# Sliding-window attention and a token mixer on one core: tails of the first batch loaded apart, scores in two-bank units, all PSUM banks shared, and a stored instruction order

## The chip, the core and the metric

The kernel runs on one core of one Trainium2 chip. A time is device microseconds (us) of one execution; the profile is one execution under the hardware profiler, and its span is some 1.8 us shorter than the time of that execution. Engines: PE (matmul), PEld (weight load, overlaps PE), ACT (ScalarE), DVE (VectorE), POOL (GpSimd), SP (the queue that issues most DMAs here). "Slow" here is a run more than 1.5% above the fastest of the same kernel. Only fast runs are compared. A ratio is the mean time of one kernel's fast runs over that of the other's fast runs of the same rounds, so it is not quite the ratio of the medians that are quoted beside it.

## The reference

Eight batches, eight heads, 576 positions, head size 64, float32 inputs.

```python
scores = q @ k.T / 8 + slopes[h] * -(i - j)        # only 0 <= i - j < 128, else -1e9
attn   = softmax(scores)
x      = (attn @ v) as [batch, 576, 512]            # heads side by side
wq, wk = x @ w_q, x @ w_k                           # 512 -> 64
mixed  = (wq @ wk.T / 8) @ x                        # over the 576 tokens
out    = relu(mixed) @ w_out
```

The 576 positions are four blocks of 128 and a *tail* of 64.

## The kernel before

Everything is an operation with a name, the engines that may run it, a priority, and what it reads and writes. A list scheduler with a cost table orders the operations when the kernel is built; the order of each engine is then fixed. Names used below: S (scores of a head pair), E (exponential), M (product with the bias table), PV (values), N (normalising), XT (transpose of x), WK, WQ, G, MX, R (the mixer; R is its relu), O and Oe (output product and its copy from PSUM).

PSUM has eight banks. They are allocated as four tiles of two banks each:

```python
pairs = [pp.tile([P, 1024], FP32, name=f"bank{i}") for i in range(4)]
def bank(b):
    return pairs[b // 2][:, 512 * (b % 2) : 512 * (b % 2) + 512]
```

The scores of a pair of heads take banks 0 to 3 as one unit; each head's exponential reads two of them. All other work but the mixing shares banks 4 to 7:

```python
def banks_for(o, t):
    ...
    if n == 4:
        return (0, 1, 2, 3) if all(ok[0:4]) else None
    if n == 2:
        return next(((b, b + 1) for b in pool if b % 2 == 0 and ok[b] and ok[b + 1]), None)
    free_ = [b for b in pool if ok[b]]
    return next(((b,) for b in free_ if not ok[b ^ 1]), (free_[0],) if free_ else None)
...
op({"PE": 0.48}, f"S{b}{c}", ..., opens=(key, 4, None), mode="R")
for i in range(2):
    op({"ACT": 0.95}, f"E{b}{c}{i}", ...)          # pt[.., i, 0:1024] = exp(pairs[i] / 8)
```

Inputs go through six load buffers (`ld`, 512 KB each), are cast to half precision by POOL, transposed by PE and copied to SBUF. The tails of all eight batches are loaded at the start, and batch 0 needs them:

```python
for b in range(NB):                                 # x: q, k, v
    nc.sync.dma_start(out=ldtail[x][16 * b : 16 * b + 16],       # 16 partitions
                      in_=srcs[x][b, :, 512:576, :].rearrange("h (g j) d -> g h (j d)", j=4))
```

The softmax here doesn't subtract the row's maximum and nothing guards it: scores larger than these inputs give would overflow.

Of the kernel before, what the change touches and what calls it, by code (L numbers as in the profile page):

```python
# [13 lines left out]
P = 128  # L15
# [13 lines left out]
PE_SWITCH = {("F", "R"): 0.12, ("R", "F"): 0.16, ("F", "C"): 0.12, ("C", "F"): 0.16,  # L29
             ("R", "C"): 0.15, ("C", "R"): 0.15}  # L30
LAT = {"PE": 0.25, "ACT": 0.12, "DVE": 0.12, "POOL": 0.15, "SP": 0.1}
MODE_PEN = 0.6
# [3 lines left out]
class Op:  # L36

# [3 lines left out]
    def __init__(self, engs, name, prio, fn, reads=(), writes=(), after=(), opens=None, psum=None,  # L41
                 mode="F", dma=0.0, lag=0.0):
        self.engs, self.name, self.prio, self.fn = engs, name, prio, fn
        self.reads, self.writes, self.after = list(reads), list(writes), list(after)
        self.opens, self.psum, self.mode, self.dma, self.lag = opens, psum, mode, dma, lag
        self.deps, self.room, self.memory = {}, set(), {}
        self.banks = self.eng = None
        self.insts = []


def plan(ops, rings):
# [25 lines left out]
    for us in users.values():  # L77
        opener = [o for o in us if o.opens][0]
        for o in us:
            if o is not opener:  # L80

                opener.deps.update({n: d for n, d in o.deps.items() if n in o.room})
                o.deps[opener.name] = o.memory[opener.name] = opener
    left = {k: len(v) for k, v in users.items()}
    bank_free, bank_user, where = [0.0] * 8, [None] * 8, {}
    n_deps = {o.name: len(o.deps) for o in ops}
    succ = {}
    for o in ops:
        for d in o.deps:
            succ.setdefault(d, []).append(o)  # L90
    engines = ("PE", "ACT", "DVE", "POOL", "SP")
    ready = {e: [] for e in engines}

    def release(o):
        for e in o.engs:
            ready[e].append(o)
    for o in ops:
        o.ready = {e: 0.0 for e in o.engs}
        if not o.deps:
            release(o)  # L100
    free = dict.fromkeys(engines, 0.0)
    mode, dma_free, t, order = "F", 0.0, 0.0, []

    def banks_for(o, t):
        _, n, pool = o.opens
        ok = [bank_user[b] is None and bank_free[b] <= t + 1e-9 for b in range(8)]
        if n == 4:
            return (0, 1, 2, 3) if all(ok[0:4]) else None
        if n == 2:
            return next(((b, b + 1) for b in pool if b % 2 == 0 and ok[b] and ok[b + 1]), None)  # L110
        free_ = [b for b in pool if ok[b]]
        return next(((b,) for b in free_ if not ok[b ^ 1]), (free_[0],) if free_ else None)

    while len(order) < len(ops):
        moved = False
        for e in engines:
            if free[e] > t + 1e-9:
                continue
            best = None
            for o in ready[e]:  # L120
                pr = o.prio + (MODE_PEN if e == "PE" and o.mode != mode else 0.0)
                if o.ready[e] > t + 1e-9 or best is not None and pr >= best[0]:
                    continue
                if o.opens and banks_for(o, t) is None:
                    continue
                best = (pr, o)
            if best is None:
                continue
            o = best[1]
            for e2 in o.engs:  # L130
                ready[e2].remove(o)
            o.eng, o.start = e, t
            if e == "PE" and o.mode != mode:
                o.start += PE_SWITCH[mode, o.mode]
                mode = o.mode
            o.end = free[e] = o.start + o.engs[e]
            o.done = o.end
            if o.dma:
                dma_free = max(o.end + 1.0, dma_free) + o.dma
                o.done = dma_free + 0.9  # L140
            if o.opens:
                where[o.psum] = banks_for(o, t)
                for b in where[o.psum]:
                    bank_user[b] = o.psum
            if o.psum:
                o.banks = where[o.psum]
                left[o.psum] -= 1
                if left[o.psum] == 0:
                    for b in o.banks:
                        bank_user[b], bank_free[b] = None, o.done + LAT[e]  # L150
            order.append(o)
            for s in succ.get(o.name, []):
                for e2 in s.engs:
                    lag = o.lag if e2 == e and not o.dma else LAT["SP" if o.dma else e]
                    s.ready[e2] = max(s.ready[e2], o.done + lag)
                n_deps[s.name] -= 1
                if n_deps[s.name] == 0:
                    release(s)
            moved = True
        if not moved:  # L160
            times = [free[e] for e in engines] + bank_free
            times += [o.ready[e] for e in engines for o in ready[e]]
            later = [x for x in times if x > t + 1e-9]
            if not later:
                raise RuntimeError("stuck: " + str([o.name for e in ready for o in ready[e]][:20]))
            t = min(later)
    order.sort(key=lambda o: o.start)
    return order


# [76 lines left out]
def steps(nc, pool, pp, q, k, v, moe_w_q, moe_w_k, moe_w_out, out):  # L247
# [5 lines left out]
    def bank(b):  # L253
# [32 lines left out]

    ptf = pt.rearrange("p a i w -> p (a i w)").bitcast(FP32)
    ldtail = [ptf[:, 2048 * i : 2048 * i + 2048].rearrange("p (h w) -> p h w", h=H) for i in range(2)]
    ldtail.append(rm.rearrange("p i c w -> p (i c w)").bitcast(FP32).rearrange(
        "p (h w) -> p h w", h=H))  # L290
    nattail = [osb[i].rearrange("p t w -> p (t w)").bitcast(F16).rearrange(
        "p (a j h d) -> p a j h d", a=2, j=4, h=4) for i in range(2)]
# [45 lines left out]
    def f_ones(eng, bk):  # L338
# [3 lines left out]
        nc.vector.memset(vtail[64:128], 0.0)  # L342

# [6 lines left out]
    op({"DVE": 1.1}, "k zero", -98, lambda eng, bk: nc.vector.memset(kTt, 0.0), writes=[("kzero", 0)])  # L350
    op({"DVE": 1.5}, "ones", -15, f_ones, writes=[("ones", 0)])
    op({"DVE": 0.3}, "zero", -14, f_zero, writes=[("zero", 0)])
    op({"DVE": 0.2}, "pads", -10, f_pads, after=["cast qt", "cast kt"], writes=[("pads", 0)])
# [16 lines left out]
    op({"POOL": 3.2}, "load w", 12, f_w, writes=[("w", 0)], dma=1.0)  # L370
# [5 lines left out]
    srcs, loads = (q, k, v), []  # L376
    for b in range(NB):
        base = b * PERIOD
        for hh in range(2):
            for x in range(3):  # L380
                pr = (base - 14 + 2 * hh * SLOT + x * 0.3, base - 9 + hh * SLOT)[x == 2]
                loads.append((pr, b, x, hh))
    for i, (pr, b, x, hh) in enumerate(sorted(loads)):
        t = ld[i % RINGS["ld"]]

        def f_load(eng, bk, b=b, x=x, hh=hh, t=t):
            src = srcs[x][b, 4 * hh : 4 * hh + 4, 0:512, :].rearrange(
                "h (g j) d -> g h (j d)", j=4)
            nc.sync.dma_start(out=t, in_=src)

        def f_cast(eng, bk, b=b, x=x, hh=hh, t=t):
            dst = vn[b % 2][:, :, 4 * hh : 4 * hh + 4, 0:64]
            if x < 2:
                dst = nat[(4 * b + 2 * hh + x) % RINGS["nat"]]
            copy(eng, dst, in_order(t))
        name = f"{'qkv'[x]}{b}{hh}"
        op({"SP": 0.45}, "ld " + name, pr - 4, f_load, writes=[("ld", i)], dma=1.4)
        engs = {"POOL": 1.1}
        if b == 0 and x < 2:
            engs = {"POOL": 1.1, "DVE": 1.1, "ACT": 0.95}  # L400
        op(engs, "cast " + name, pr, f_cast, reads=[("ld", i)] + [("ones", 0)] * (x == 2),
           writes=[("vn", b) if x == 2 else ("nat", 4 * b + 2 * hh + x)])
    for x in range(3):
        for b in range(NB):
            def f_loadt(eng, bk, x=x, b=b):
                (nc.scalar if eng == "ACT" else nc.sync).dma_start(
                    out=ldtail[x][16 * b : 16 * b + 16],
                    in_=srcs[x][b, :, 512:576, :].rearrange("h (g j) d -> g h (j d)", j=4))
            op({("ACT", "SP", "SP")[x]: 0.45}, f"ld {'qkv'[x]}t{b}", (-50, -17.5, -12.5)[x], f_loadt,
               writes=[("ldt", x)], dma=0.35)  # L410

        def f_castt(eng, bk, x=x):
            for hh in range(2):
                src = in_order(ldtail[x][:, 4 * hh : 4 * hh + 4])
                if x < 2:
                    copy(eng, nattail[x][:, hh], src)
                else:
                    copy(eng, vntail[:, :, 4 * hh : 4 * hh + 4, 0:64], src)
        name = f"{'qkv'[x]}t"
        op({"POOL": 2.2, "DVE": 2.2} if x < 2 else {"POOL": 2.2}, "cast " + name,  # L420
           (-13, -12.8, -5)[x], f_castt, reads=[("ldt", x), ("ones", 0)], writes=[("natt", x)])
    for b in range(NB):
        for kb in range(NT):
            def f_hop(eng, bk, b=b, kb=kb):
                src = vn[b % 2][32 * kb : 32 * kb + 32].rearrange("p j h d -> p j (h d)")
                nc.sync.dma_start(out=vt[b % 2][:, kb, :], in_=src)
            op({"SP": 0.45}, f"hop{b}{kb}", b * PERIOD - 4.5 + SLOT, f_hop, reads=[("vn", b)],
               writes=[("vt", b)], dma=0.4)

# [315 lines left out]
```

## Time and profile before

| | before |
|---|---|
| time, median of 2 runs | 232.6 us (231.56 and 233.64) |
| span of the profile | 230.8 us |
| first WK result ("wkn") copied out, batch 0 | 63.7 us |
| last "wkn", batch 7 | 212.9 us |
| mean step from one "wkn" to the next | 21.3 us |
| last "wkn" to the end | 17.9 us |

"wkn" is the result of the mixer's first projection; its DVE copy marks the point where a batch's attention is done. The next lines are from the page's second part: the span in 40 slices of 5.8 us; digits are busy tenths, DMA is the busy share of the DMA engines, GB/s what they moved.

```profile
PE   0012615687676787498859977886989598774560
...
DMA  6999999999999976997899730182065026015026
GB/s 142 179 162 182 213 262 347 288 320 323 352 347 344 348 223 162 358 349 208 250 354 296 181 98 3 44 196 83 4 151 127 0 73 160 0 27 158 0 71 156
```

The DMA engines are shown busy from the second slice on, yet the first five slices move about half of what later ones move, and PE is busy for little more than a quarter of the time until slice 8 (46 us; slices are counted from 0). The windows view gives each engine's busy time in the three stretches, start, steady part and end:

```profile
core 0: us, PE busy (x) PEld busy (x) DVE busy (x) ACT busy (x) POOL busy (x), PEclk, DMA share, GB/s
0.00:64.00 64.00, 26.96 (x361) 22.03 (x362) 31.86 (x53) 32.83 (x42) 28.56 (x40) 0.92 1.11 253
64.00:213.00 149.00, 115.98 (x1527) 76.54 (x1521) 85.03 (x145) 93.61 (x150) 35.05 (x30) 0.92 0.60 175
213.00:230.80 17.80, 6.94 (x38) 2.78 (x38) 0.92 (x2) 5.95 (x14) 0.00 (x0) 0.88 0.29 74
```

In the steady part no engine is full: PE is busy for 116 of 149 us. The tile view of the banks for ACT in that stretch says what ACT's idle time ended with (us, times):

```profile
its engine sat idle before it (us, times) until:
  PE bank L186: 34.2, 30
  DVE xT L186: 13.0, 8
```

The end of the timeline (start, duration, engine, operation, and in brackets the idle time before it and what ended that):

```profile
218.29 1.89 PE L186 MATMUL bank<-wout_sb,rm 128*128 128x512 f16 x8 [1.60 <-ACT rmt L186]
...
220.21 0.59 ACT L186 COPY osb<-bank 128x512 f32<-128x512 f32 x1 [1.37 <-PE bank L186]
220.85 1.02 PE L186 MATMUL bank<-wout_sb,rmt 128*128 128x512 f16 x4 [0.67 <-ACT osb L186]
221.91 0.59 ACT L186 COPY osb<-bank 128x512 f32<-128x512 f32 x1 [1.11 <-PE bank L186]
```

Two output products (x8) are done by 220.2.

### The profile page before, as it was taken

The page shows a single profiled execution, that of the slowest core. Times are in us where ns is not written, and L with a number is a line of the kernel's source. Part 1 is how long each engine was busy: PE and PEld are TensorE (multiplying, and loading weights), DVE is VectorE, ACT ScalarE, POOL GpSimd, SP SyncE. Part 2 cuts the span into 40 slices and gives each one's busy share as a digit, 9 for nine tenths or more (in the row PEclk, how much of TensorE's full clock was granted, in tenths as well). Part 3 has the DMA queues.
Part 4 walks back from the last instruction along what each step waited for, and adds up shares of the span by engine and source line. Part 5 has one row for each costly group of instructions (what it writes and reads, how often), then busy time and mean ns, then how long its engine had stood idle before and what let it go on. Part 6 is the DMA issues. An engine that isn't in the chain of part 4 may idle for free.

```text
span 230.8 us, 4775 instructions
## 1 busy us (share of the span) xinstructions
PE 149.9 (65%) x1920; PEld 101.4 (44%) x1920; DVE 117.8 (51%) x198; ACT 132.4 (57%) x206; POOL 63.6 (28%) x69
## 2 busy tenths in 40 slices
PE   0012615687676787498859977886989598774560
PEld 0011504476545465255545655563556356333220
DVE  6101727459893387323780786386278648244000
ACT  0059654745655566925582749854785895821531
POOL 6400524747575660670093035000000000000000
PEclk9999999659998899959995999999799999799996
DMA  6999999999999976997899730182065026015026
GB/s 142 179 162 182 213 262 347 288 320 323 352 347 344 348 223 162 358 349 208 250 354 296 181 98 3 44 196 83 4 151 127 0 73 160 0 27 158 0 71 156
DMA packets 41414, 43.51 MB, mean 189 GB/s; under 512 B 4016, under 2 KB 36784, under 8 KB 41392
## 3 DMA queue, kind: packets, MB, share of 16 engines
q1 hardware_dynamic: 38656, 41.50, 65.5%
q0 software_dynamic: 1584, 0.66, 3.1%
q10 hardware_dynamic: 1152, 1.05, 2.9%
q8 instruction: 15, 0.25, 0.4%
q14 instruction: 7, 0.06, 0.1%
HBM read 29.62 MB, written 9.44 MB: 169 GB/s over the span
## 4 chain that ended last, share of the span: by engine, by line
PE 38%; ACT 20%; DMA 18%; DVE 17%; issue 3%; POOL 1%; SPq 0%; ACTq 0%; DVEq 0%
PE bank L186 38%; DMA pt<-in_k_dram 9%; ACT pt L186 5%; ACT rm L186 5%; ACT osb L186 4%; ACT kT L186 4%; DVE x L186 4%; DVE pt L186 4%; DMA ld<-in_q_dram 3%; DVE xT L186 3%; DMA ld<-in_k_dram 3%; DMA rm<-in_v_dram 3%; DVE qT L186 3%; DVE wkn L186 2%; DVE inv L186 1%
## 5 line engine op out<-in xcount | busy, mean ns | idle before, releaser
L186 ACT ACTIVATE pt<-bank 128x1024 f16<-128x1024 f32 x64 | 63.0, 1030 | 22.0 <-PE bank L186 21.6
L186 DVE TENSOR_TENSOR pt<-pt,table 128x2048 f16<-128x2048 f16 x32 | 41.5, 1297 | 11.1 <-ACT pt L186 10.9
L186 PE MATMUL bank<-ident,nat 128*128 128x128 f16 x256 | 22.9, 246 | 35.1 <-ACT nat L186 16.7
L186 PE MATMUL bank<-wout_sb,rm 128*128 128x512 f16 x128 | 37.3, 423 | 10.3 <-ACT kT L186 5.1
L186 POOL CAST nat<-ld 128x1024 f16<-128x1024 f32 x28 | 34.3, 1228 | 32.5 <-PE bank L186 14.5
L186 PEld LDWEIGHTS <-nat 128*128 128x128 f16 x256 | 18.9, 110 | 38.0 <-ACT nat L186 16.9
L186 ACT COPY osb<-bank 128x512 f32<-128x512 f32 x32 | 18.6, 592 | 26.2 <-PE bank L186 19.6
L186 DVE COPY xT<-bank 128x576 f16<-128x576 f16 x32 | 14.5, 454 | 31.7 <-PE bank L186 24.4
L186 DVE TENSOR_TENSOR x<-bank,inv 128x640 f16<-128x640 f32 x32 | 26.4, 824 | 1.1
L186 POOL CAST vn<-ld 128x1024 f16<-128x1024 f32 x16 | 19.4, 1212 | 22.1 <-DMA vt<-vn 11.0
L186 PEld LDWEIGHTS <-pt 128*128 128x128 f16 x576 | 22.6, 103 | 5.4 <-issue 4.0
L186 PE MATMUL bank<-vt,pt 128*128 128x65 f16 x512 | 23.8, 201 | 1.1 <-ACT osb L186 0.7
L186 PEld LDWEIGHTS <-rm 128*128 128x128 f16 x128 | 12.9, 105 | 24.2 <-issue 15.3
L186 PE MATMUL bank<-ident,x 128*128 128x128 f16 x160 | 15.6, 233 | 10.9 <-DVE x L186 3.7
L186 ACT COPY kT<-bank 128x1024 f16<-128x1024 f16 x16 | 16.7, 1043 | 10.2 <-PE bank L186 4.7
L186 PE MATMUL bank<-qT,kT 64*128 64x256 f16 (+1 forms) x256 | 21.1, 282 | 1.0 <-ACT pt L186 0.9
L186 DVE COPY qT<-bank 128x512 f16<-128x512 f16 x32 | 12.0, 418 | 18.8 <-PE bank L186 18.8
L186 PEld LDWEIGHTS <-x 128*128 128x128 f16 x160 | 11.4, 104 | 19.1 <-issue 9.3
L186 ACT ACTIVATE rm<-bank 128x512 f16<-128x512 f32 x32 | 19.3, 620 | 0.6 <-PE bank L186 0.6
L186 PEld LDWEIGHTS <-kT 64*128 64x128 f16 x320 | 14.5, 101 | 8.8 <-issue 5.2
L186 DVE RECIPROCAL inv<-bank 128x10 f32<-128x10 f32 x32 | 6.9, 217 | 15.6 <-PE bank L186 15.1
L186 PE MATMUL bank<-wqT,gm 64*128 64x256 f16 x64 | 8.4, 295 | 7.0 <-ACT rmt L186 2.5
(49 smaller groups left out, 136.7 us busy)
## 6 DMA issues: line engine op xcount, KB each, us to landing
ld<-in_q_dram SPq DMA_DIRECT2D x16, 512.0 KB, 7.3
ld<-in_k_dram SPq DMA_DIRECT2D x16, 512.0 KB, 7.8
ld<-in_v_dram SPq DMA_DIRECT2D x16, 512.0 KB, 7.3
out_dram<-osb SPq DMA_DIRECT2D x64, 128.0 KB, 2.3
vt<-vn SPq DMA_DIRECT2D x32, 130.0 KB, 3.9
pt<-in_q_dram ACTq DMA_DIRECT2D x8, 128.0 KB, 9.6
pt<-in_k_dram SPq DMA_DIRECT2D x8, 128.0 KB, 9.4
rm<-in_v_dram SPq DMA_DIRECT2D x8, 128.0 KB, 6.9
```

The costliest lines, as they stand in the source:

```text
L186: r = call(*a, **k)
```

## The change

Its intent: let batch 0 start without the tails of all batches; let the scores double-buffer and use whatever PSUM is free; divide the copies out of PSUM between ACT and DVE; and store an order found by a search instead of running the list scheduler. Core of the diff, cuts marked:

```diff
-def plan(ops, rings):  ... list scheduler ...
+def planned(ops):                       # the order and the banks are a stored string
+    for item in PLAN.split():           # "281A6": operation 281 on ACT; digit: first bank
+        n, e, b = re.fullmatch(r"(\d+)([PADGS])(\d?)", item).groups()
+        ...
 # scores
-            op({"PE": 0.48}, f"S{b}{c}", ..., opens=(key, 4, None), mode="R")
-            # E{i}: pt[.., i, 0:1024] from two fixed banks
+            for u in range(2):          # key blocks 0-1, then 2-4, of both heads
+                op({"PE": 0.24}, f"S{b}{c}{u}", ..., opens=(key, 2), mode="R")
+                # E{u}: pt[.., both heads, 512 columns] from any pair
 # batch 0's own tails, 0.4 MB
+        (nc.scalar if eng == "ACT" else nc.sync).dma_start(
+            out=ldn[x][0:64], in_=srcs[x][0, :, 512:576, :].rearrange("h s d -> s h d"))
 # the other tails: with batch 1, one head of all batches per transfer, 128 partitions
-            out=ldtail[x][16 * b : 16 * b + 16],
-            in_=srcs[x][b, :, 512:576, :].rearrange("h (g j) d -> g h (j d)", j=4))
+            out=t[:, h, :], in_=srcs[x][:, 4 * hh + h, 512:576, :].rearrange(
+                "b (g j) d -> g b (j d)", j=4))
-    op({"POOL": 3.2}, "load w", 12, f_w, ..., dma=1.0)
+    op({"POOL": 3.2}, "load w", 12, f_w, after=["cast k01"], ..., dma=4.0)
 # DVE may evict too: relu R, outputs Oe and OTe, k
-            op({"ACT": 0.62}, f"R{b}{db}", ...)
+            op({"ACT": 0.59, "DVE": 0.75}, f"R{b}{db}", ...)
 # each POOL cast waits for the last bias product M
+            tc.add_manual_dep(o.insts[0], bias.insts[0].name, ..., reason="port")
```

## The prediction

> **What bounds the kernel before** (timeline, unless said).
>
> 1. *Start, 0 to 64 us* (64: first mixing projection, "wkn", of batch 0). DMA binds: its engines are shown 99% busy from slice 1 on. But slices 0 to 4 move 142 to 213 GB/s, later ones 320 to 350. The packets show why: while the 64-row tails of all eight batches stream (24 transfers of 128 KB, each into 16 partitions), a 1024-byte packet takes 92 to 112 ns (median); from 30 us on, 48 to 58. The tails hold up everything: first exponential at 29.9 us, second pair at 37.7, first value product at 48.6.
> 2. *Steady, 64 to 213 us*: "wkn" at 64, 89, 112, 134, 156, 175, 194, 213: 21.3 us a batch. PE is busy 116 of these 149 us and idles 33, 25 of them in gaps over 0.5 us. ACT waits for PE's banks 34 us in 30 waits (tile view of the banks). ACT and DVE are 55 to 75% busy (windows view). No engine is full: they wait on each other in turn. One cause: a pair's scores take four fixed banks, and both exponentials (1.03 us each) must end before the next pair's scores start; everything else shares the other four.
> 3. *End, 213 to 231 us*: output of the last batch, mostly serial.
>
> **The change.** Engine work stays: 64 exponentials of 1024 columns, 32 bias products, the same matmuls plus 8 small transposes. By my count the tiling mode changes 99 times before, 95 after (the Trainium skill, "TensorEngine Tiling (Array Packing)", Key Properties: a mode change drains the array), so smaller score units cost nothing there. Removed: batch 0's wait for all tails (0.4 MB first, the rest with batch 1, spread over 128 partitions, so I expect full-rate packets); the early weight load; the bank split; ACT's monopoly of evictions (9 of 32 relus, 8 of 36 output copies, 3 of 16 k evictions go to DVE). Added: each POOL cast waits for the last bias product, which took 1.34 us while POOL ran and 1.22 after; at most 3 us are in this.
>
> **Cost.** *Start*: "wkn" of batch 0 needs about 10.4 MB; at 330 GB/s plus 2 to 3 us that is 34 us, then cast, transposes, eviction, scores, exponential: 6. ACT needs 10 us of tables (from 6 us) + 16.5 (exponentials) + 4 (evictions): also near 38. I expect 42: minus 22. *Steady*: DVE needs about 15.5 us a batch, ACT 14.5, PE 16.7. A searched order with free banks should reach 18.5, against 21.3: 7 x 2.8 = minus 20. *End*: copies and relus over two engines: 15 instead of 17.8: minus 3. Sum: 42 + 130 + 15 = 187 us span, plus 1.8 between span and time, plus 1 for what a fixed order loses.
>
> Predicted: 190 us, range 180 to 202. Faster by over 2%: 0.97, within 2%: 0.02, slower: 0.01.
>
> **What would show it.** Right: slices 1 to 5 above 280 GB/s; first exponential at 14 to 18 us; "wkn" of batch 0 at 38 to 46; 17.5 to 19.5 us between "wkn"s; ACT's waits for banks between first and last "wkn" halved; last "wkn" to end 14 to 16 us. Wrong: tails still at 90 ns a packet; a steady period near 21 us with PE idle 20%, which would say that banks were not what held it.
>
> **What would make it wrong.** The steady period is the weakest term: each microsecond there is 7. The denser PE may be granted a lower clock (0.92 on average now), or the order may stall on late DMA in batches 1 and 2.

## The result, and the profile after

190.7 us, median of 2 fast runs (190.62 and 190.79); ratio to before 0.8199, 95% interval 0.8041 to 0.8357. The total came within 1 us of the prediction. Its three parts did not:

| part of the span | before | predicted | after |
|---|---|---|---|
| start: to the first "wkn" | 63.7 | 42 | 49.3 |
| steady: first to last "wkn" | 149.2 (21.3 a batch) | 130 (18.5) | 117.1 (16.7) |
| end: last "wkn" to the end | 17.9 | 15 | 22.6 |

The lines that answer to those of before, the slices of 4.7 us now:

```profile
PE   0339549548686999978888999988988988976740
...
DMA  4996999999799879999889999998664216273564
GB/s 134 289 338 176 253 276 292 237 250 273 183 323 329 219 218 340 307 320 328 265 215 357 320 309 294 324 332 274 163 154 119 55 33 194 47 185 104 150 173 121
```

The windows view of the three stretches:

```profile
0.00:49.00 49.00, 27.32 (x320) 20.49 (x320) 26.98 (x47) 29.63 (x40) 25.57 (x41) 0.80 0.95 250
49.00:166.00 117.00, 102.29 (x1547) 71.11 (x1546) 95.19 (x173) 83.00 (x124) 36.88 (x37) 0.98 0.80 242
166.00:189.10 23.10, 11.96 (x64) 4.65 (x62) 2.49 (x5) 7.59 (x16) 0.00 (x0) 0.93 0.56 143
```

PE does the work of the steady part (about the same number of matmuls, 1547 and 1527) in 117 us and is busy for 102 of them. So of the 32 us that went, 18 were idle time of PE (33 to 15) and 14 busy time (116 to 102), with a granted clock of 0.98 and not 0.92 in that stretch; section 1 comes back to the clock. ACT's waits between first and last "wkn":

```profile
its engine sat idle before it (us, times) until:
  PE bank L163: 18.7, 25
  DVE osb L163: 4.7, 1
  DVE xT L163: 3.2, 4
```

The wait for PE's banks is about halved, from 34.2 to 18.7 us. The start stayed at 250 GB/s although its packets were now fast. What the DMA queue on SP waited for in the first 50 us:

```profile
SPq L163 <- POOL vn L163: 4.0, 2, 3.6
SPq L163 <- POOL vntail L163: 3.6, 1, 3.6
SPq L163 <- DVE nat L163: 3.3, 1, 3.3
SPq L163 <- DMA ld<-in_q_dram: 3.0, 2, 2.1
SPq L163 <- POOL nat L163: 2.2, 2, 1.6
```

POOL's and DVE's casts (13.1 us of these) are what frees a load buffer. So for 13 of the first 50 us the loads stood still for lack of buffers, not for lack of bandwidth. The end, finally:

```profile
174.43 1.89 PE L163 MATMUL bank<-wout_sb,rm 128*128 128x512 f16 x8 [0.61 <-DVE osbt L163]
176.36 0.58 ACT L163 COPY osb<-bank 128x512 f32<-128x512 f32 x1 [1.78 <-PE bank L163]
...
176.99 1.02 PE L163 MATMUL bank<-wout_sb,rm 128*128 128x512 f16 x4 [0.67 <-ACT osb L163]
178.05 0.58 ACT L163 COPY osb<-bank 128x512 f32<-128x512 f32 x1 [1.11 <-PE bank L163]
178.69 1.02 PE L163 MATMUL bank<-wout_sb,rmt 128*128 128x512 f16 x4 [0.67 <-ACT osb L163]
179.75 0.58 ACT L163 COPY osb<-bank 128x512 f32<-128x512 f32 x1 [1.11 <-PE bank L163]
```

These products stand alternately in banks 2 and 3. The semaphore values in the built program, condensed, PE's counter in brackets:

```
PE   product O(6,2) -> bank 2
PE   product O(7,1) -> bank 3                 [1912]
ACT  copy of bank 2            waits for PE [1912]     the product in bank 3
PE   product O(7,0) -> bank 2  waits for ACT's copy of bank 2              [1916]
ACT  copy of bank 3            waits for PE [1916]     the product in bank 2
```

The copy of bank 2 waits for a product in bank 3 and the other way round. The two banks are halves of one PSUM tile, and the waits come out as if the tile were one piece of memory. By a count over the whole program, 159 of the 522 waits between instructions that touch PSUM have their other end in the partner bank only; before the change it is 167 of 512. Some of these also carry data through SBUF (46 of the 159 and 56 of the 167 go to an instruction that reads what the other one wrote), the rest guard nothing. I call the rest *false waits*.

### The profile page after: what moved, and what is told of

It is laid out like the page before. It is cut to its first block, busy times and chain, and to the rows that moved or that the text cites. A ratio compares the mean times of both kernels' runs of the same rounds, so it can differ in the third digit from the quotient of the medians.

```text
span 189.1 us, 4795 instructions
## 1 busy us (share of the span) xinstructions
PE 141.6 (75%) x1928; PEld 96.3 (51%) x1928; DVE 124.7 (66%) x225; ACT 120.2 (64%) x180; POOL 62.5 (33%) x76
## 4 chain that ended last, share of the span: by engine, by line
PE 34%; DVE 24%; DMA 16%; ACT 13%; issue 4%; SPq 3%; POOL 1%; ACTq 1%; DVEq 0%; POOLq 0%
PE bank L163 34%; DVE pt L163 6%; DVE x L163 5%; DMA ldn<-in_q_dram 4%; ACT kT L163 4%; DVE xT L163 4%; DMA ld<-in_k_dram 4%; ACT osb L163 3%; DMA vt<-vn 3%; DMA out_dram<-osb 3%; SPq L163 3%; DVE qT L163 3%; ACT rm L163 3%; DMA ld<-in_q_dram 2%; DVE wkn L163 2%
## 5 line engine op out<-in xcount | busy, mean ns | idle before, releaser
L163 PE MATMUL bank<-wout_sb,rm 128*128 128x512 f16 x128 | 31.7, 379 | 4.7 <-ACT osb L163 1.3
L163 PE MATMUL bank<-ident,nat 128*128 128x128 f16 x288 | 26.1, 248 | 9.8 <-POOL nat L163 2.7
L163 ACT COPY osb<-bank 128x512 f32<-128x512 f32 x26 | 14.9, 589 | 23.0 <-PE bank L163 14.5
L163 PEld LDWEIGHTS <-nat 128*128 128x128 f16 x288 | 21.2, 111 | 14.7 <-issue 8.2
L163 PE MATMUL bank<-qT,kT 64*128 64x256 f16 (+1 forms) x256 | 23.2, 277 | 5.0 <-ACT kT L163 1.5
L163 POOL CAST vn<-ld 128x1024 f16<-128x1024 f32 x16 | 16.8, 1057 | 20.1 <-DMA ld<-in_v_dram 11.5
L163 ACT COPY kT<-bank 128x1024 f16<-128x1024 f16 x13 | 13.4, 1028 | 9.4 <-PE bank L163 8.9
L163 PE MATMUL bank<-ident,x 128*128 128x128 f16 x160 | 13.0, 222 | 4.9 <-DVE qT L163 3.6
L163 ACT ACTIVATE rm<-bank 128x512 f16<-128x512 f32 x23 | 13.8, 604 | 4.0 <-PE bank L163 3.8
L163 PE MATMUL bank<-x,wkn 128*64 128x512 f16 x80 | 10.1, 380 | 1.5 <-DVE osb L163 0.9
```

Of the source, the lines that this page charges most:

```text
L163: r = call(*a, **k)
```

## The experiments

All kernels gave correct results. Fast means below are means of the fast runs.

| run | what | fast runs | fast mean | ratio to before |
|---|---|---|---|---|
| before_spread | before, tails over 128 partitions | 2 | 222.4 | none given (231.8 for before) |
| before_nopair | before without false waits | 2 | 203.6 | none given |
| list_old | tails apart (with the later weight load and POOL's wait of the change); scores, banks, evictions and scheduler as before | 2 | 210.8 | 0.9088 (0.8956 to 0.922) |
| list_old_np | the same without false waits | 4 | 198.3 | 0.8596 (0.845 to 0.8741) |
| list_new | the change, order by the list scheduler | 2 | 198.6 | 0.8618 (0.847 to 0.8767) |
| list_new_np | the same without false waits | 4 | 181.4 | none given |
| the change | | 2 | 190.7 | 0.8199 (0.8041 to 0.8357) |
| noport | the change without POOL's added wait | 2 | 190.4 | 0.8212 (0.8107 to 0.8317) |
| nopair | the change without false waits | 3 | 177.6 | 0.7659 (0.7569 to 0.7748) |
| plan_act_np | nopair, evictions back on ACT | 4 | 182.4 | 0.7801 (0.7736 to 0.7866) |
| plan_split_np | nopair, scores in banks 0-3 only | 4 | 198.3 | none given |
| plan_pair_np | the same, one pair at a time | 4 | 210.1 | none given |
| np_ld8 | nopair with eight load buffers | 6 | 174.8 | 0.7585 (0.7521 to 0.7649) |

No ratio is given for some runs, mostly because only one run of before in their rounds was fast (228.8 us, the others 233 to 237). The differences read from those runs are larger than that, except the 3.8 us between `list_new_np` and `nopair`. The rows come from different chips, so a difference of a few us between two rows is not exact.

### 1. The false waits taken away

The edit goes after the order is made. It declares, for users of the two different banks of a pair on different engines, that there is nothing to wait for; waits that carry data stay. Operations that hold two banks are left out; by the count above, 53 of 568 waits still have their other end in the partner bank only in `nopair`, and 41 of 563 in `before_nopair`. `before_nopair` has the same edit on the kernel before.

```diff
     drop_implied(tc, order)
+    apart(tc, order)
+def apart(tc, order):
+    last = {}
+    for o in order:
+        if not o.banks or len(o.banks) > 1:
+            continue
+        for d in last.get(o.banks[0] ^ 1, [])[-12:]:
+            if d.name not in o.deps and d.eng != o.eng:
+                for i in o.insts:
+                    for j in d.insts:
+                        tc.declare_no_dep(i, j, reason="another bank")
+        last.setdefault(o.banks[0], []).append(o)
```

> The changed kernel, with the waits taken away that the built program has between users of the two different banks of one PSUM pair (the data never meet). In the trace of the changed kernel the last five output products each wait 0.67 us for the copy before, because the copy of one bank starts only when the product in the other bank of its pair has ended. Theory (these waits are false and cost time): those five gaps go, minus 3.3 us at the end, and a few us more in the middle: 183 to 188 us against 190.7. Rival (the engines are full and the waits only show where the slack is): at the end 3 us less at most, in all 188 to 190.7.

Measured: 177.6 us against 190.7, a gain of 13 where I had thought of 3 to 8. "wkn" of batch 0 came at 46.9 us, the steady step was 16.1 us, the end 18.0 us (its profile fell in a run 1% above the fast mean, so these are a little long). The end shows it best; these lines are from the timeline of the run with eight load buffers (section 5), which has the same end:

```profile
160.56 2.76 PE L163 MATMUL bank<-wout_sb,rm 128*128 128x512 f16 x12
...
161.63 0.58 ACT L163 COPY osb<-bank 128x512 f32<-128x512 f32 x1 [0.23 <-PE bank L163]
...
162.50 0.58 ACT L163 COPY osb<-bank 128x512 f32<-128x512 f32 x1 [0.28 <-PE bank L163]
163.16 1.03 PE L163 MATMUL bank<-wout_sb,rmt 128*128 128x512 f16 x4
163.36 0.58 ACT L163 COPY osb<-bank 128x512 f32<-128x512 f32 x1 [0.28 <-PE bank L163]
```

PE no longer has any bracket: it runs product after product, and each copy follows its own product. In the changed kernel's end PE stood for 5.1 us in eight gaps: four of 0.67 us before the last output products (the expectation says five) and four of 0.58 to 0.68 us before earlier products. All eight are gone here, and the end went from 22.6 to 18.0 us.

> The kernel before without the false waits between the two banks of a pair. There all work but the scores sits in banks 4 to 7, so in two pairs, and a bank whose partner is in use is taken first. Theory (the false waits cost it as much as they cost the new kernel, 10 to 13 us): 219 to 224 us against 232, and PE's gaps smaller. Rival (they became dear only through the sharing of all banks): 229 to 233 us.

Measured: 203.6 us, against 228.8 for the one fast run of before in these rounds and 231.8 on average before them. So the false waits cost the old kernel some 25 to 28 us, more than they cost the new one (13). The theory named their kind rightly and put their size at half. The trace has the steady step at 17.4 us in place of 21.3, while the first "wkn" stays at 62.7 and the end at 18.0 us. Its steady stretch in the windows view:

```profile
63.00:185.00 122.00, 105.91 (x1520) 70.19 (x1516) 84.79 (x145) 92.08 (x150) 35.78 (x31) 0.97 0.72 217
```

So **of the 4.6 us a batch by which the change shortened the steady part, 3.9 could be had in the old kernel by dropping waits alone.** My prediction named the fixed banks and the exponentials that must end as the cause of these gaps.

A rival is the granted clock, which is 0.97 in this stretch and 0.92 in the kernel before; PE is busy for 106 us with as many matmuls, not 116. But `list_old` (section 2), with its false waits in place, was granted 0.99 in its steady stretch (44 to 190 us), and there PE still idled for 34 us and the step was 20.9 us. So a higher clock alone does not shorten the step; why the clock differs is not shown. In the end of `before_nopair` the three gaps of 0.67 us are gone as well, but the clock there was 0.70 (0.88 before) and PE was busy for 10.7 us with 46 matmuls (6.9 us with 38 before), which took the gain back.

### 2. The tails: how many partitions, and loading them apart

```diff
-    out=ldtail[x][16 * b : 16 * b + 16], in_=srcs[x][b, :, 512:576, :]...("h (g j) d -> g h (j d)")
+    out=ldtail[x][:, b, :],              in_=srcs[x][:, b, 512:576, :]...("b (g j) d -> g b (j d)")
     # cut: the two places that read the tails follow the new layout
```

> The kernel before, only that each tail transfer fills 4 rows of 16 tokens in all 128 partitions (one head of all batches) and not 16 partitions (one batch, all heads); number, bytes and 1 KB packets stay. Theory (the 16 partitions are what made the packets slow): packets of 46 to 60 ns in the first 30 us and not 92 to 112, first exponential at 22 to 26 us and not 29.9, wkn of batch 0 at 54 to 59 and not 64, 223 to 228 us. Rival (the slow packets come of too many small loads or of the cold start of the run): packets still about 90 ns, 231 to 233 us.

Measured: 222.4 us against 231.8, a little better than the expected 223 to 228. A 1024-byte packet took these medians, by stretches of 5 us:

```
                0-5   5-10  10-15  15-20  20-25  25-30 us
before           46    102    112     96     92    100 ns
before_spread    46     59     59     46     46     47 ns
```

The first exponential came at 24 us and not at 29.9, "wkn" of batch 0 at 57 and not at 63.7. The Trainium skill, "SBUF — State Buffer", Door 1, says that DMA bandwidth depends on how many of 16 ports the partitions of a transfer reach, and by its table 16 neighbouring partitions reach four. This run agrees in kind: the bytes, the number of transfers and the packet size are the same, the partitions changed (and with them which tails go in one transfer), and packets became about twice as fast.

`list_old` keeps this and loads batch 0's tails apart, all as in the change, but has the scores, banks, evictions and scheduler of before:

```diff
-            for u in range(2): ... op({"PE": 0.24}, f"S{b}{c}{u}", opens=(key, 2)) ...
+            op({"PE": 0.48}, f"S{b}{c}", ..., opens=(key, 4, None))     # as before
-   opens=(key, 1)          +   opens=(key, 1, range(4, 8))             # as before
-   order = planned(ops)    +   order = the list scheduler of before
```

> The tails apart alone: the changed kernel's loads and batch 0's own tails, but the scores in four fixed banks, the other work in the other four, evictions on the engines of before and the order from the list scheduler of before. Theory (the start is worth its own share and the steady period keeps 21 us): wkn of batch 0 at 45 to 50 us, 20.5 to 21.5 us a batch after, 214 to 219 us. Rival (what the start gains is given back, as the next batches wait for their loads): 224 to 232 us.

Measured: 210.8 us, ratio 0.9088, below the expected 214 to 219: half of the whole gain. "wkn" of batch 0 came at 43.8, the steady step was 20.9. Of the lead of 20 us over the kernel before at the first "wkn", 15 were left at the second (73.6 and 88.8).

### 3. The same without false waits

> The tails-apart-alone kernel (210.7 us fast) without the false waits: four fixed banks for a pair's scores, the rest in the other four, evictions and scheduler of before. It is to be compared with the list-ordered new kernel without false waits (181.4). Theory (most of what the new bank structure gained in the steady period was fewer and cheaper false waits; without them two-bank units and sharing bring little): 183 to 189 us. Rival (units, sharing and split evictions have a worth of their own, about the 21 us that the loads left): 196 to 204 us.

Measured: 198.3 us. My theory, that little would be left for the bank structure once the false waits are gone, fell: the list-ordered new kernel is at 181.4, so 17 us stay between them. But the trace says that not all of the 17 is banks. In `list_old_np` the first "wkn" came at 42.4 and the third at 97.7, no earlier than in `before_nopair` (98.0): the whole lead was lost on the way. The DMA queue on SP issues in a fixed order, and between 58.2 and 68.9 us it issued no load at all, only tail moves, stores and value moves:

```profile
57.84 0.38 SPq L196 DMA_DIRECT2D ld<-in_k_dram  x1
59.24 0.54 SPq L196 DMA_DIRECT2D vtail<-vntail  x1
59.88 3.37 SPq L196 DMA_DIRECT2D out_dram<-osb  x4
63.36 3.39 SPq L196 DMA_DIRECT2D vt<-vn  x4
66.84 1.98 SPq L196 DMA_DIRECT2D out_dram<-osb  x4
68.86 0.43 SPq L196 DMA_DIRECT2D ld<-in_v_dram  x1
```

POOL then sat idle for 8.4 us for want of a load, and from 75 to 92 us the DMA engines ran at 354 GB/s to catch up (at a granted clock of 0.70 for PE). How much of the 17 us is banks and units and how much is such accidents of the list order, these runs do not tell.

### 4. What the order is worth

`list_new` and `list_new_np` are the change with the list scheduler of before in place of the stored order.

> All of the change but its order, with the false waits: the list scheduler of before on the new operations. Without false waits this order was only 4 us behind the searched one (181.4 against 177.6). Theory (the search, made by running or by a model that has the waits, partly went around them; a list that knows nothing of them pays more): 195 to 206 us, so the order is worth 5 to 15 us where the false waits stand. Rival (the order's worth is the same 4 us with and without them): 193 to 196 us.

> All of the change but its order: the list scheduler of the kernel before orders the new operations, with shared banks, two-bank units and free choice of the evicting engine, and without the false waits. Theory (the searched order has a share of its own, as half of the gain is still to be placed after the loads took the other half): 186 to 196 us. Rival (once banks are free any sensible order does): 177 to 182 us.

Measured: 198.6 and 181.4 us. With the false waits the stored order is worth 7.9 us (198.6 to 190.7), as the theory said, without them 3.8 (181.4 to 177.6; the two come with one fast run of before in one of them, so this small difference is rough). The expectation for `list_new_np`, 186 to 196, missed: with banks free and no false waits, an order made in the old way comes within about 2% of the searched one by these times. Its rival was right. The profile of `list_new` fell in a slow run (clock 0.777), so nothing is read from its trace.

The next two runs were to tell units from sharing by forcing the stored order into the old bank split. An operation that finds no bank waits and those behind it go on:

```diff
+    ok = [x for x in (range(0, 4) if o.name[0] == "S" else range(4, 8)
+                      if o.name[:2] != "MX" else range(0, 8)) if owner[x] is None]
+    # plan_pair_np only: a pair's scores open only when the pair before has both its E placed
```

> As the run with one pair at a time, but two units of two banks each may come from different pairs, still in banks 0 to 3 only. Theory (the unit of two banks matters more than the sharing): half or less of the loss of the run with one pair at a time, 179 to 184 us. Rival (the sharing matters and the unit doesn't): the same loss as that run.

> To be compared with the run without the false waits (177 us fast), which has the same searched order and engines: the scores of one pair at a time in banks 0 to 3, everything else but the mixing in banks 4 to 7, as in the kernel before; an operation that finds no bank waits in the order and those behind it go on. Theory (two-bank units in shared banks are a good part of what the steady period gained): 186 to 193 us, steady 17.5 to 18.5 us a batch, and ACT waiting for PE's banks more. Rival (the order and the split evictions did it, and banks were not what held the kernel): 177 to 181 us.

Measured: 198.3 and 210.1 us, 21 and 32 us above `nopair`, far beyond what both theories allowed. `plan_pair_np` is slower than the old kernel with its own order (`before_nopair`, 203.6) under the same restriction. So these runs measure mostly what happens to an order that was made for other banks, and they don't say what a bank is worth. They are inconclusive for the question that they were sent for.

### 5. Evictions, POOL's wait, load buffers

`plan_act_np`: in the stored order, 19 operations change from D to A, same places and banks ("596D0" to "596A0" and so on).

> The searched order, banks and places of the run without false waits (177.6 us fast, ratio to before 0.766), but the 19 evictions that the change gives to DVE (9 relus, 6 output copies, 2 tail copies, one copy of G, one of k) go back to ACT, each at its place in the order. ACT's busy time goes from 120 to about 134 us, DVE's from 126 to about 111. Theory (splitting the evictions is a part of the gain of its own): 181 to 187 us, ratio 0.78 to 0.80. Rival (ACT has room, the split matters little): 177 to 179.5 us, ratio under 0.775.

Measured: 182.4 us, ratio 0.7801 against 0.7659 (the intervals touch at 0.774). In this order the split evictions are worth about 4.8 us, as the theory said; an order searched for evictions on ACT alone was not tried.

`noport`: the added wait of the POOL casts is left out.

```diff
-        if o.name.startswith("cast") and o.eng == "POOL" and bias:
-            tc.add_manual_dep(o.insts[0], bias.insts[0].name, ..., reason="port")
```

> The changed kernel without the wait of each POOL cast for the last bias product. Theory (the wait is about neutral): POOL's 31 us of waits for DVE go, the bias products grow from 1.24 us to about 1.3, 189 to 192 us. Rival A (the wait protects DVE): bias products 1.35 us and more, 193 us or more. Rival B (it delays the casts of batches 1 and 2 and with them the loads, and is part of why the first projection came at 49 us and not at 42): first projection at 45 to 47 us and 186 to 188.5 us.

Measured: 190.4 us, the same: the theory's time, though the bias products grew by more than it said. The wait does what it is for: with it a bias product took 1.24 us on average and a cast 1.03 us, without it 1.41 and 1.20 (the profile of `noport` fell in a run 2% above its fast ones; the two engines' own durations are what counts here). The Trainium skill, "SBUF — State Buffer", Who interferes with whom, says that a DVE instruction with two SBUF inputs and a GpSimd instruction that reads SBUF shut each other out; the durations agree. In `noport` 20 of the 32 bias products overlapped a POOL cast and took 1.53 us on average (at most 2.06), the 12 others 1.21; with the wait 7 overlapped (1.35) and 25 did not (1.21). What the wait saves in durations it seems to cost in idle time: POOL waited 31 us for DVE in the changed kernel. "wkn" of batch 0 came at 49.5 without it and at 49.3 with it, so it did not delay the start.

`np_ld8`: `nopair` with eight load buffers, numbered in the order in which the stored plan issues the loads (six in that numbering cannot be built with that order, so number and numbering are not told apart).

```diff
-RINGS = {"ld": 6, ...
+RINGS = {"ld": 8, ...
-    for i, (pr, b, x, hh) in enumerate(pieces):
+    for pr, b, x, hh in pieces:
+        i = issued.index(name of the piece)
```

> A try to beat both: the searched order without the false waits (177.6 us fast) and with eight load buffers in place of six, taken in the order in which the loads are issued. Without the false waits POOL waits 43 us for loads, and PE 13 us for POOL's casts. Theory (the load queue stands behind buffers that are not yet read): 172 to 176 us, wkn of batch 0 at 42 to 46 us. Rival (the loads are bound by the DMA engines or by the casts' own order): 176.5 to 178.5 us.

Measured: 174.8 us, six fast runs from 174.0 to 175.6: **8% under the change and 24% under the kernel before.** Most of this is the false waits: the step from `nopair` (177.6) is under 2%, and the intervals of the two ratios overlap. "wkn" of batch 0 came at 43.3 us and not at 46.9. The DMA queue's waits in the first 50 us:

```profile
SPq L163 <- POOL vn L163: 5.0, 1, 5.0
SPq L163 <- DMA ld<-in_v_dram: 1.8, 2, 1.3
SPq L163 <- POOL vntail L163: 1.6, 1, 1.6
SPq L163 <- DMA ld<-in_q_dram: 0.9, 2, 0.7
SPq L163 <- POOL nat L163: 0.8, 2, 0.4
```

POOL's and DVE's casts hold the queue for 7.4 us here, against 13.1 in the changed kernel and 11.3 in `nopair`. The slices:

```profile
PE   0277579468877989979983999999999999999940
```

PE is nearly full from slice 22 on.

## Why the prediction was right or wrong

- **The total was right (190 against 190.7) by luck: errors cancelled.** Start: predicted minus 22, measured minus 14.4. Steady: minus 20, measured minus 32. End: minus 3, measured plus 4.7.
- **Start.** The mechanism was right: packets fell to 46 to 59 ns, the first exponential came at 16.8 us (expected 14 to 18), and `before_spread` and `list_old` show the two parts of it. The step that was mis-sized is "10.4 MB at 330 GB/s": the start moved 250 GB/s. I took packet speed for transfer rate. Of slices 1 to 5, which I wanted above 280 GB/s, two were. The loads waited for buffers and casts; eight buffers, newly numbered and without false waits, brought the first "wkn" to 43.3 us, near the 42 where I had put it.
- **Steady.** I said that a searched order with free banks should reach 18.5 us; it reached 16.7 on average (single steps run from 8.5 to 24.3, from 18.8 to 25.1 before). My estimate of PE's own need, 16.7 us of busy time a batch, was too high to be a floor: `np_ld8` steps at 15.9, and in the changed kernel PE is busy for 14.6 us a batch. PE's denser work was not granted a lower clock, as I feared, but a higher one in the profiles taken, 0.98 against 0.92 in that stretch. ACT's waits for banks fell from 34.2 to 18.7 us, as said. But the reason that I gave for the idle time, the fixed banks and the exponentials that must end, was at best a part of it: dropping the false waits alone takes the old kernel from 21.3 to 17.4 us a batch. I had the line "ACT waits for DVE xT" before me and did not ask why.
- **End.** "Copies and relus over two engines: 15 us" failed. The stored order leaves more output products after the last "wkn" (64 matmuls against 38 there), and the false waits put PE and ACT in turns. Without them the end is 18.0 us with the larger work.
- **Evictions.** That the split matters is shown for this order: about 4.8 us, with the false waits gone.
- **POOL's wait.** "At most 3 us are in this" held: 190.4 and 190.7.
- **Tiling modes.** 99 changes before and 95 after, by the same count in the new trace, so the smaller score units indeed cost nothing there. No run here times a change of mode.
- **Where the 42 us went.** In the order in which one can build them, with the false waits in place: tails apart 231.8 to 210.8, the new operations with the old scheduler to 198.6, the stored order to 190.7. Without the false waits the same steps read 203.6, 198.3, 181.4, 177.6. The steps don't add up to the same in both rows, since a gain at one point is partly lost at the next: tails apart is worth 21 us in the first row and 5 in the second, where the lead was lost again while a load of batch 3 stood in the queue. Open: the share of two-bank units against that of shared banks.

## What to carry to other kernels

When an engine waits for another that has nothing to do with its data, look up which semaphore value it waits for: a dependency tracked more coarsely than the memory it guards shows in the trace as alternation of two engines and as gaps of one fixed size, and taking it out was worth more in the kernel before (25 to 28 us) than any one part of the change there (21 at most). Before crediting a new structure with the idle time that it removed, remove the waits by themselves once, in the old kernel as well. And read transfer rate, not packet time, when estimating a load phase: the queue that issues the loads, and the buffers that they need, can be the limit while every packet is fast.

## What the Trainium skill lacked or had wrong

- "PSUM — Partial Sum Buffer", the rule to guard PSUM with semaphores by bank and quadrant: agreed with. Kernels without most of the waits between the two banks of a pair gave correct results in all their runs. What the page lacks is the cost of guarding more than that: 13 us of 190.7 in the changed kernel, 25 to 28 of some 230 in the kernel before.
- "Perfetto Trace Analysis", Optimization Strategy: it says that a gap which keeps repeating "can mean there isn't enough SBUF/PSUM for the next tile to be allocated". Here the repeated gap of 0.67 us at the end came with most banks free; another cause, waits on the partner bank, is missing from that sentence.
- "SBUF — State Buffer", Door 1: agreed with in kind (packets of 92 to 112 ns into 16 partitions, 46 to 59 into 128). No page gives the packet's duration by number of ports reached, which is how it shows in a trace.
- No page says that a load phase with fast packets can still run at 250 GB/s because the issuing queue stands behind buffers: eight buffers in a new numbering in place of six, with the false waits gone, moved the first projection from 46.9 to 43.3 us.
